# A tuned two-layer GELU block: early loads in order of need on one queue, remainder rows used last, first tiles copied ahead

**Chip, cores, metric.** One core of one Trainium2 chip. The time is the device time of one execution in microseconds (us); the profile's span is about 1.3 us shorter. Medians and ranges are of several executions. Times inside a profile are us from the start of its span.

## The reference

```python
B, S, D, F = 1, 2048, 448, 1792          # all bf16
def reference(x, w1, b1, w2, b2):
    h = jnp.einsum("bsd,df->bsf", x, w1) + b1
    h = gelu_tanh(h)
    return jnp.einsum("bsf,fd->bsd", h, w2) + b2
```

D = 448 is three tiles of 128 rows and a remainder of 64; F is 14 tiles ("F-tiles"). The remainder rows of w1 ("w1r") are a load of their own.

## The kernel before

The sequence is cut into four blocks of 512 rows. For the first block x is loaded as it is (two loads, `x(0)` and `x(2)`, of two tiles each) and turned by TensorE; the other blocks come through transposing loads. Layer 1 of the first block runs in two halves of 256 columns, each in seven steps of two F-tiles. A step has two parts, which use the two 64-row halves of the array crosswise; TensorE runs them in the order 0a, 1a, 0b, (b1 and tiles 2, 3 turned), 2a, 1b, 3a, 2b and so on. In the code, names such as `("w1r", 1)` are events that a load raises and a matmul waits for.

```python
W1CUTS = (0, 2, 6, 14)                       # w1 in chunks of 2, 4 and 8 F-tiles
load_x(0); load_w1(0); load_x(2); load_w1(1); load_w1(2)     # all issued on SyncE
load_w2(0, 7); load_w2(7, 14)
# ... b2, and 12 transposing loads for blocks 1 to 3, also on SyncE
load_w1r(0, 1, ("w1r", 0))                   # on ScalarE: for F-tiles 0, 1
load_w1r(1, NPAIR, ("w1r", 1))               # on ScalarE: the rest
# ... ScalarE's table load; GpSimd makes the identity and loads b1

def turn(t, engines):
    # VectorE: xr[t] = remainder columns of x, twice side by side   (after x)
    # TensorE: four transposes into PSUM, the fourth from xr[t]
    # VectorE: evacuation of the four into xT
    ...
# layer 1, one step (cut)
def part_a():
    for k in range(KT + 1):                  # k == KT is w1r: 8 matmuls
        for lo in (0, 1):
            after = need if k == 0 else []
            after = after + [("w1", w1_of(2 * j + lo)) if k < KT else ("w1r", min(j, 1))]
            mm(lo, lo, k, k == 0, False, after, turned if k == KT and lo else None)
def part_b():
    for k in range(KT):                      # 6 matmuls
        ...
# start
warm(7); turn(0, "vector"); turn(1, "vector"); warm(1)      # warm: matmuls on ones, for the clock
```

## Time and profile before

| | kernel before |
|---|---|
| time, first three executions | 102.14 us (102.1 to 102.41) |
| span of the profiled execution | 100.8 us |
| step 0 of layer 1 starts | 5.77 |
| second w1 chunk used first | 8.07 |
| w1r of the later steps used first | 9.90 |
| step 2 starts | 12.56 |
| layer 2 of the first block starts | 24.15 |
| half clock, as recorded | 10.03 to 16.86 |

How to read it: from 24.15 on TensorE runs without a gap, so a change at the start is worth exactly what it moves this point. The lines are in the prediction.

### The profile page before, as it was taken

Reading aid. Unit: us, or ns where it says so; the run is one execution under the profiler, and the core shown is the slowest. Engines: PE = TensorE matmul, PEld = TensorE weight load, DVE = VectorE, ACT = ScalarE, POOL = GpSimd, SP = SyncE. Lnnn points to the kernel's source line nnn. Section 1 sums busy time; section 2 is a strip of 40 time slices with the busy share of each in tenths; the row PEclk is TensorE's granted clock in tenths of the full one; section 3 lists DMA queues with packets and bytes.
Section 4 is the critical chain, followed back from the end, with each engine's and each line's share of the span. In section 5 each row is a group of like instructions: output and inputs, shape, how many; then the busy total and the mean of one; then the engine's idle time right before and its main releaser. Section 6 shows DMA issues by size and latency. Waiting matters only on the chain.

```text
span 100.8 us, 2247 instructions
## 1 busy us (share of the span) xinstructions
PE 94.4 (94%) x1020; PEld 51.3 (51%) x1020; DVE 12.4 (12%) x29; ACT 39.1 (39%) x73; POOL 2.4 (2%) x9
## 2 busy tenths in 40 slices
PE   6862899999999999999999999999999999999991
PEld 2411477887455444445455444445454444457790
DVE  0210310100001440000004500000034100000421
ACT  0500335999100018887000068891000388850001
POOL 6300000000000000000000000000000000000000
PEclk9999556999999999999999999999999999999999
DMA  2899999555520330000001210000002200000032
GB/s 60 216 291 361 380 287 160 66 106 102 65 48 0 95 94 0 0 3 0 7 0 46 90 47 0 7 0 0 7 0 91 91 0 7 0 0 0 0 98 91
DMA packets 13321, 7.34 MB, mean 73 GB/s; under 512 B 7936, under 2 KB 12928, under 8 KB 13312
## 3 DMA queue, kind: packets, MB, share of 16 engines
q1 hardware_dynamic: 12288, 6.97, 26.5%
q10 hardware_dynamic: 960, 0.23, 1.0%
q8 instruction: 8, 0.13, 0.6%
q0 software_dynamic: 64, 0.00, 0.0%
q14 instruction: 1, 0.01, 0.0%
HBM read 3.79 MB, written 1.84 MB: 56 GB/s over the span
## 4 chain that ended last, share of the span: by engine, by line
PE 87%; DMA 7%; ACTq 2%; DVE 1%; issue 0%
PE u L228 44%; PE u L276 42%; DMA w1r<-in_w_dram 7%; ACTq L128 2%; PE u L180 1%; DVE xT L187 0%; DVE out_sb L315 0%; PE u L194 0%; DVE xr L174 0%; DVE b_f L196 0%; PE u L283 0%
## 5 line engine op out<-in xcount | busy, mean ns | idle before, releaser
L248 ACT ACTIVATE g<-u,b_f 128x512 bf16<-128x512 f32 (+1 forms) x70 | 37.2, 600 | 47.6 <-PE u L228 41.0
L228 PE MATMUL u<-xT,w_sb 64*128 64x512 bf16 (+1 forms) x420 | 45.0, 349 | 1.4 <-DMA w_sb<-in_w_dram 1.3
L276 PE MATMUL u<-w_sb,g 64*128 64x448 bf16 (+1 forms) x504 | 43.2, 328 | 0.0
L276 PEld LDWEIGHTS u<-w_sb,g 64*128 64x128 bf16 x504 | 24.2, 94 | 18.5
L228 PEld LDWEIGHTS u<-xT,w_sb 64*128 64x128 bf16 x420 | 21.0, 99 | 19.4 <-DMA w_sb<-in_w_dram 1.7
L300 DVE TENSOR_TENSOR out_sb<-u,b_bc 128x448 bf16<-128x448 f32 x14 | 8.1, 619 | 67.9 <-PE u L276 67.9
L228 PE MATMUL u<-xT,w1r 64*128 64x512 bf16 (+1 forms) x70 | 12.3, 350 | 1.3 <-DMA w1r<-in_w_dram 1.3
L228 PEld LDWEIGHTS u<-xT,w1r 64*128 64x128 bf16 x70 | 3.6, 100 | 4.5 <-DMA w1r<-in_w_dram 1.6
L166 PE MATMUL u<-const-bfloat16-1.0 128*128 128x512 bf16 x8 | 3.8, 625 | 0.8 <-PEq L384 0.8
L318 ACT CAST out_sb<-u 128x224 bf16<-128x224 f32 x1 | 0.3, 346 | 9.0 <-PE u L276 9.0
L150 ACT ACT_TABLE_LOAD x1 | 1.3, 1283 | 3.3 <-issue 3.3
L166 PEld LDWEIGHTS u<-const-bfloat16-1.0 128*128 128x128 bf16 x8 | 1.0, 132 | 2.1 <-issue 2.1
L180 PE MATMUL u<-ident,xn 128*128 128x128 bf16 x12 | 2.0, 312 | 0.0
L187 DVE COPY xT<-u 128x512 bf16<-128x512 bf16 x4 | 1.7, 425 | 2.0 <-PE u L180 2.0
L180 PE MATMUL u<-ident,xr 128*128 128x128 bf16 x4 | 1.2, 292 | 0.6 <-DVE xr L174 0.6
L180 PEld LDWEIGHTS u<-ident,xn 128*128 128x128 bf16 x12 | 1.4, 139 | 0.6 <-issue 0.6
L360 DVE COPY xT<-xT 64x512 bf16<-64x512 bf16 x3 | 0.9, 289 | 5.7 <-DMA xT<-in_x_dram 5.7
L180 PEld LDWEIGHTS u<-ident,xr 128*128 128x128 bf16 x4 | 0.5, 114 | 1.4 <-DVE xr L174 1.4
L174 DVE COPY xr<-xn 128x128 bf16<-128x128 bf16 x4 | 0.7, 187 | 2.4 <-DMA xn<-in_x_dram 2.4
L196 DVE CAST b_f<-u 128x14 f32<-128x14 bf16 x1 | 0.2, 173 | 5.4 <-PE u L194 5.4
L308 DVE TENSOR_TENSOR out_sb<-u,b_bc 128x448 bf16<-128x448 f32 x1 | 0.6, 625 | 1.7 <-PE u L276 1.7
L158 POOL DMA_DIRECT2D b1n<-in_b_dram x1 | 0.7, 652 | 0.2 <-issue 0.2
(15 smaller groups left out, 3.4 us busy)
## 6 DMA issues: line engine op xcount, KB each, us to landing
out_dram<-out_sb SPq DMA_DIRECT2D x16, 112.0 KB, 1.7
w_sb<-in_w_dram SPq DMA_DIRECT2D x2, 784.0 KB, 9.8
w_sb<-in_w_dram SPq DMA_DIRECT2D x1, 768.0 KB, 7.7
xn<-in_x_dram SPq DMA_DIRECT2D x2, 224.0 KB, 3.7
w_sb<-in_w_dram SPq DMA_DIRECT2D x1, 384.0 KB, 5.8
w_sb<-in_w_dram SPq DMA_DIRECT2D x1, 192.0 KB, 2.8
w1r<-in_w_dram ACTq DMA_DIRECT2D x2, 96.0 KB, 6.3
xT<-in_x_dram SPq DMA_TRANSPOSE x12, 4.1
```

The costliest lines, as they stand in the source:

```text
L128: pr.dma("scalar", lambda e, lo=lo: e.dma_start(w1r[lo * H:(lo + 1) * H, j0:j1, :], w1rv[:, j0:j1, lo, :]), event)
L150: pr.op("scalar", lambda e: e.activation(junk[:, :], one, ACT.Gelu_apprx_tanh))
L158: pr.dma("gpsimd", lambda e: e.dma_start(b1n[0:NFT, :], b1.rearrange("(c p) -> c p", p=P)), "b1n", after=["b1z"])
L166: pr.op("tensor", lambda e: e.matmul(unit[3][:, 1, 0:cols], lhsT=ones_w, rhs=ones_m[:, 0:cols], start=True, stop=True))
L174: pr.op("vector", lambda e: e.tensor_copy(xr[:, t, :].rearrange("p (two h) -> p two h", two=2), xn[:, t, D3:D].unsqueeze(1).broadcast_to([ ...
L180: pr.op("tensor", lambda e, k=k, src=src: e.transpose(stage(t)[:, k * P:(k + 1) * P], src, ident[:, :]), after=need, event=("xt", t) if k ...
L187: return e.copy(o, i) if engines == "scalar" else e.tensor_copy(o, i)
L228: pr.op("tensor", lambda e: e.matmul(unit[u][:, lo, 0:n], lhsT=lhsT, rhs=rhs, start=first, stop=fin), after=after, event=event)
L248: pr.op("scalar", lambda e, lo=lo, ft=ft: e.activation(g[:, ft, c0:c1], unit[u][:, lo, 0:n], ACT.Gelu_apprx_tanh, bias=b1_f[:, ft:ft + 1], ...
L276: pr.op("tensor", lambda e: e.matmul(unit[u][:, lo, 0:n], lhsT=g[rows, ft, j * P:(j + 1) * P], rhs=w2_sb[rows, ft, d0:d0 + n], start=first ...
L300: pr.op("vector", lambda e, lo=lo, j=j: e.tensor_tensor(out=out_sb[:, j, :], in0=unit[u][:, lo, 0:D], in1=b2_bc[:, :], op=ALU.add), after= ...
L360: pr.op("vector", lambda e, cs=cs: e.tensor_copy(xT[0:H, KT, cs], xT[H:P, KT, cs]), after=[("xT", c + 1)], event=("xTd", c + 1))
```

## The change

All early loads go on the SyncE queue in the order in which TensorE needs them. w1r is no longer split by step, only by array half (the halves change places), comes behind the first six F-tiles, and is used last in a step's second part. The last w1 load, of eight F-tiles, becomes two of four. Both xr copies are made before the first evacuation. The b1 load and the one-row b2 load go from GpSimd to ScalarE. Core of the diff (renamed lines, some removed lines and the moved b2 load are cut):

```diff
-        W1CUTS = (0, 2, 6, 14)
+        W1CUTS = (0, 2, 6, 10, 14)
...
-        def load_w1r(j0, j1, event):
+        def load_w1r():
             for lo in (0, 1):
-                pr.dma("scalar", lambda e, lo=lo: e.dma_start(
-                    w1r[lo * H:(lo + 1) * H, j0:j1, :], w1rv[:, j0:j1, lo, :]), event)
+                pr.dma("sync", lambda e, lo=lo: e.dma_start(
+                    w1r[(1 - lo) * H:(2 - lo) * H, :, :], w1rv[:, :, lo, :]), "w1r")
...
         load_x(0)
         load_w1(0)
+        load_w1(1)
+        load_w1r()
         load_x(2)
-        load_w1(1)
         load_w1(2)
+        load_w1(3)
         load_w2(0, 7)
         load_w2(7, 14)
...
-        load_w1r(0, 1, ("w1r", 0))
-        load_w1r(1, NPAIR, ("w1r", 1))
...
-        pr.dma("gpsimd", lambda e: e.dma_start(b1n[0:NFT, :], b1.rearrange("(c p) -> c p", p=P)), "b1n",
+        pr.dma("scalar", lambda e: e.dma_start(b1n[0:NFT, :], b1.rearrange("(c p) -> c p", p=P)), "b1n",
                after=["b1z"])
...
+        def turn(tiles, copier):
+            for t in tiles:
+                ...  xr copy of tile t
+            for t in tiles:
+                ...  four transposes of tile t, then its evacuation
...
             def part_a():
+                for k in range(KT):
+                    for lo in (0, 1):
+                        after = (need if k == 0 else []) + [("w1", w1_of(2 * j + lo))]
+                        mm(lo, lo, k, k == 0, False, after, turned if k == KT - 1 and lo else None)
+
+            def part_b():
                 for k in range(KT + 1):
                     for lo in (0, 1):
-                        after = need if k == 0 else []
-                        after = after + [("w1", w1_of(2 * j + lo)) if k < KT else ("w1r", min(j, 1))]
-                        mm(lo, lo, k, k == 0, False, after, turned if k == KT and lo else None)
+                        fin = k == KT
+                        mm(lo, 1 - lo, k, False, fin, [turned] if k == 0 else ["w1r"] if fin else [],
+                           ("h", c, 2 * j + lo, c0) if fin else None)
...
-        turn(0, "vector")
-        turn(1, "vector")
+        turn((0, 1), "vector")
```

More of the change, by code (lines that the diff above doesn't have):

```diff
@@ L146, in bass_standalone__dense_activation_gelu__prompt_kernel @@
                     xT[:, slot, c * SC:(c + 1) * SC], x2[c * SC:(c + 1) * SC, d0:d0 + P], transpose=True), ("xT", c))
-        load_w1r(0, 1, ("w1r", 0))
-        load_w1r(1, NPAIR, ("w1r", 1))
-        pr.op("scalar", lambda e: e.activation(junk[:, :], one, ACT.Gelu_apprx_tanh))
         pr.op("gpsimd", lambda e: e.memset(ident[:, :], 0.0), event="ident0")
@@ L157, in bass_standalone__dense_activation_gelu__prompt_kernel @@
         pr.op("vector", lambda e: e.memset(b1n[:, :], 0.0), event="b1z")
-        pr.dma("gpsimd", lambda e: e.dma_start(b1n[0:NFT, :], b1.rearrange("(c p) -> c p", p=P)), "b1n",
+        pr.dma("scalar", lambda e: e.dma_start(b1n[0:NFT, :], b1.rearrange("(c p) -> c p", p=P)), "b1n",
                after=["b1z"])
+        pr.op("scalar", lambda e: e.activation(junk[:, :], one, ACT.Gelu_apprx_tanh))
         busy = {}
@@ L170, in stage, with evac @@
             return unit[t // 2][:, t % 2, 0:2 * P].bitcast(BF16)
-        def turn(t, engines):
-            a = t - t % 2
-            pr.op("vector", lambda e: e.tensor_copy(
-                xr[:, t, :].rearrange("p (two h) -> p two h", two=2),
-                xn[:, t, D3:D].unsqueeze(1).broadcast_to([P, 2, H])), after=[("x", a)], event=("xr", t))
-            for k in range(KT + 1):
-                src = xn[:, t, k * P:(k + 1) * P] if k < KT else xr[:, t, :]
-                need = ["ident", ("x", a)] if k < KT else [("xr", t)]
-                pr.op("tensor", lambda e, k=k, src=src: e.transpose(
-                    stage(t)[:, k * P:(k + 1) * P], src, ident[:, :]),
-                    after=need, event=("xt", t) if k == KT else None)
-            def evac(e):
-                o = xT[:, :, t * P:(t + 1) * P]
-                i = stage(t).rearrange("p (k s) -> p k s", k=KT + 1)
-                return e.copy(o, i) if engines == "scalar" else e.tensor_copy(o, i)
-            pr.op(engines, evac, after=[("xt", t)], event=("xT0", t))
-            busy[(t // 2, t % 2)] = ("xT0", t)
+        def turn(tiles, copier):
+            for t in tiles:
+                pr.op("vector", lambda e, t=t: e.tensor_copy(
+                    xr[:, t, :].rearrange("p (two h) -> p two h", two=2),
+                    xn[:, t, D3:D].unsqueeze(1).broadcast_to([P, 2, H])), after=[("x", t - t % 2)], event=("xr", t))
+            for t in tiles:
+                for k in range(KT + 1):
+                    src = xn[:, t, k * P:(k + 1) * P] if k < KT else xr[:, t, :]
+                    need = ["ident", ("x", t - t % 2)] if k < KT else [("xr", t)]
+                    pr.op("tensor", lambda e, t=t, k=k, src=src: e.transpose(
+                        stage(t)[:, k * P:(k + 1) * P], src, ident[:, :]),
+                        after=need, event=("xt", t) if k == KT else None)
+                def evac(e, t=t):
+                    o = xT[:, :, t * P:(t + 1) * P]
+                    i = stage(t).rearrange("p (k s) -> p k s", k=KT + 1)
+                    return e.copy(o, i) if copier == "scalar" else e.tensor_copy(o, i)
+                pr.op(copier, evac, after=[("xt", t)], event=("xT0", t))
+                busy[(t // 2, t % 2)] = ("xT0", t)
         def turn_b1():
@@ L233, in part_a @@
                 need += [("xT0", t) for t in range(c0 // P, c1 // P)] if c == 0 else [("xT", c), ("xTd", c)]
+                for k in range(KT):
[3 more added lines that the diff above has]
+            def part_b():
                 for k in range(KT + 1):
                     for lo in (0, 1):
-                        after = need if k == 0 else []
-                        after = after + [("w1", w1_of(2 * j + lo)) if k < KT else ("w1r", min(j, 1))]
-                        mm(lo, lo, k, k == 0, False, after, turned if k == KT and lo else None)
-            def part_b():
-                for k in range(KT):
-                    for lo in (0, 1):
-                        fin = k == KT - 1
-                        mm(lo, 1 - lo, k, False, fin, [turned] if k == 0 else [],
+                        fin = k == KT
+                        mm(lo, 1 - lo, k, False, fin, [turned] if k == 0 else ["w1r"] if fin else [],
                            ("h", c, 2 * j + lo, c0) if fin else None)
@@ L338, in bass_standalone__dense_activation_gelu__prompt_kernel @@
         pr.op("gpsimd", lambda e: e.memset(b2_z[:, :], 0.0), event="b2z0")
-        pr.dma("gpsimd", lambda e: e.dma_start(b2_z[H:H + 1, :], b2.unsqueeze(0)), "b2z", after=["b2z0"])
+        pr.dma("scalar", lambda e: e.dma_start(b2_z[H:H + 1, :], b2.unsqueeze(0)), "b2z", after=["b2z0"])
         warm(NWARM)
-        turn(0, "vector")
-        turn(1, "vector")
+        turn((0, 1), "vector")
         warm(NFILL)
@@ L348, in bass_standalone__dense_activation_gelu__prompt_kernel @@
                 turn_b1()
-                turn(2, "vector")
-                turn(3, "vector")
+                turn((2, 3), "vector")
         for j in range(NPAIR):
```

## The prediction

> **What bounds the kernel now.** I read the chain of waits first, then the groups, then the first 26 us in order of time. The chain:
>
> ```profile
> PE 87%; DMA 7%; ACTq 2%; DVE 1%; issue 0%
> PE u L228 44%; PE u L276 42%; DMA w1r<-in_w_dram 7%; ACTq L128 2%; PE u L180 1%; DVE xT L187 0%; DVE out_sb L315 0%; PE u L194 0%; DVE xr L174 0%; DVE b_f L196 0%; PE u L283 0%
> ```
>
> TensorE sets the end, but the first tenth of the span is the load of the w1 remainder rows (issued on the ScalarE queue, L128), and the matmuls hang behind it. From 24.3 us on the chain alternates between pieces of 10.58 us (layer 1, 98 matmuls) and 10.59 us (layer 2, 112), without a gap; the change has nothing to win there. The start, from the timeline (start, length, engine):
>
> ```profile
> 5.05 0.63 PE L166 MATMUL u<-const-bfloat16-1.0 128*128 128x512 bf16 x1
> 5.77 0.82 PE L228 MATMUL u<-xT,w_sb 64*128 64x256 bf16 x6
> 8.07 0.50 PE L228 MATMUL u<-xT,w_sb 64*128 64x256 bf16 x6 [1.29 <-DMA w_sb<-in_w_dram]
> 9.90 0.31 PE L228 MATMUL u<-xT,w1r 64*128 64x256 bf16 x2 [1.33 <-DMA w1r<-in_w_dram]
> 12.56 0.82 PE L228 MATMUL u<-xT,w_sb 64*128 64x256 bf16 x6
> 14.88 1.49 PE L228 MATMUL u<-xT,w_sb 64*128 64x256 bf16 x12
> 17.38 0.82 PE L228 MATMUL u<-xT,w_sb 64*128 64x256 bf16 x12
> 24.15 2.05 PE L276 MATMUL u<-w_sb,g 64*128 64x448 bf16 x20
> ```
>
> Two DMA waits of 1.3 us stand in the first two steps. Less obvious: twelve matmuls take 1.49 us at 14.88 and 0.82 us at 17.38. That is the clock (columns: PE, weight loads, DVE, ACT and POOL busy, then PEclk, DMA share, GB/s):
>
> ```profile
> 7.50:10.00 2.50, 0.60 (x8) 0.32 (x10) 0.00 (x0) 0.00 (x0) 0.00 (x0) 1.00 1.06 361
> 10.00:12.50 2.50, 2.15 (x17) 1.08 (x15) 0.80 (x4) 0.84 (x2) 0.00 (x0) 0.51 1.09 380
> 12.50:15.00 2.50, 2.50 (x25) 1.78 (x26) 0.42 (x1) 0.73 (x2) 0.00 (x0) 0.50 1.30 291
> 15.00:17.50 2.50, 2.50 (x34) 1.88 (x32) 0.00 (x0) 1.31 (x4) 0.00 (x0) 0.63 0.86 168
> ```
>
> After the idle stretch the clock is halved, and "busy" hides it. The trace's clock records give the edges: full from 6.62, half from 10.03 to 16.86, full afterwards. Before 6.62 there is no record (the view shows 1.00), yet the 0.63 us filler and the six matmuls in 0.82 us at 5.77, against 0.50 us for six at 8.07, show half clock there too. So the waits cost twice: their own time, and 6.83 us of half clock after them.
>
> **What the Trainium skill says.** (1) "TensorE: Matmul & The Clock Gate", Part 1: the clock is half or full, judged over free-running windows of 3413 ns. The trace agrees: the edges lie 3.41 and 6.83 us apart. So the grid here is 3.20, 6.62, 10.03, 13.44, 16.86. (2) "DMA: Bandwidth & Descriptors", Queues, rings and completion order: each engine takes turns between queue rows, packet by packet. The trace agrees: from 5.0 to 6.5 us the packets of the second w1 chunk (1024 B, 46 ns each) alternate with w1r's (256 B, 18 ns) almost one for one. (3) The same page, Issuing engines are not separate DMA queues: a second issuer saves only issue time. So moving w1r to SyncE should lose no bandwidth and gives the order back.
>
> **The change, part by part.** Times are from the span's start.
>
> 1. Copying ahead. Now the second xr copy comes behind the first evacuation (4.72), TensorE waits for it 0.30 us, the second evacuation ends at 5.71 and step 0 starts at 5.77. With both xr copies first (two of 0.19 from 3.37) the eight transposes run through from 3.72 at the 0.105 us pitch seen there and end near 4.75; evacuations 4.38 to 4.80 and 4.82 to 5.24 (0.42 each). Step 0 starts at 5.30: 0.47 us earlier.
>
> 2. Order of loads. SyncE issues every 0.46 to 0.5 us, so the second w1 chunk (F-tiles 2 to 5, 384 KB) is its third issue, at 1.66 instead of 2.18. Its first packets now came at 4.37, behind x(2) and sharing with w1r, its last at 7.20, and TensorE got it at 8.06. In the new order it follows chunk 0, whose packets end at 3.5: 384 packets over 16 engines are 24 each, times 46 ns is 1.1 us, so data to 4.6; with the 0.45 to 0.8 us from last packet to landing that the present loads show, it lands at 5.1 to 5.4. Then w1r: 896 packets, 56 per engine, times 18 ns is 1.0 us, data to 5.7, landed by about 6.3 (now 9.85). Then x(2): 8 per engine times 74 ns is 0.6 us; but both x loads have slow first packets (up to 1.5 us in the second), so landed 6.9 to 8.0, say 7.4. The two 4-tile chunks behind take 1.1 us each and land near 8.5 and 9.6.
>
> 3. w1r last. A step's first part shrinks from 8 to 6 matmuls, its second grows from 6 to 8; the count stays 14. Step 1's first part no longer needs w1r. Only the last pair of step 0's second part does. Steps 0a and 1a (three pairs each at half clock, 0.213 a pair, from 256 columns) run 5.30 to 5.94 and 5.94 to 6.58; 0b (four pairs) 6.58 to 7.05, w1r being there already.
>
> 4. b1 transpose and tiles 2, 3. Today it is 1.78 us from the b1 transpose (10.78) to step 2 (12.56), of which the second xr copy behind an evacuation is 0.7. In the new order: b1 transpose 7.05, b1 copy to 7.5, two xr copies to 7.9, last transpose near 8.0. Step 2 starts at about 8.15 if x(2) is there by 7.4: 4.4 us earlier than now.
>
> 5. Clock. In the window 3.20 to 6.62 TensorE would stream 0.72 (warm-up) + 0.85 (transposes) + 0.43 (filler) + 1.28 (0a, 1a) = 3.28 of 3.41 us. The present kernel streams about 2.85 there and gets full clock at 6.62; in 10.03 to 13.44 it streams about 2.45 and does not. So the new one gets it at 6.62 as well. In the next window it would stream 0.43 + 0.5 + 1.9, about 2.8 us, against 0.5 now, so it should keep the clock. Then the 174 matmuls from step 2 to the end of the first layer 1 take 12.43 steps of 14, each 0.765 us (the spacing of the twelves after 17.38): 9.5 us instead of 11.6. That is another 2.1 us.
>
> Sum: layer 2 starts at 8.15 + 9.5 = 17.65 instead of 24.15, 6.5 us earlier. I take off 0.3 for a unit not yet freed (the evacuation of tile 3 ends at about 8.9, when step 3 wants its unit, and the gelus at 0.384 us each, two a step, are just 0.77 against TensorE's 0.765). Everything after is the same gap-free chain. 102.14 - 6.2 = 95.9; with the lean of the rivals below I say **96.1**.
>
> Beside the path: b1 and b2 loads move from GpSimd to ScalarE. b1n is issued near 1.0, lands near 4, needed at 7.05; the table load (1.28 us) ends near 3, long before the first gelu at 7.6. The w2 load now ends at 14.4 and has three us to spare. The transposing loads of the second x block, now done by 18.76, are needed at 17.65 + 10.6 = 28.2. Both stay hidden.
>
> **The rivals.** (a) The wait moves on: w1r's small packets or x(2)'s slow ones hold step 2 until 9 to 9.5. For it: x(2) took 2.5 us for 0.6 us of packets; against: part of that lay beside w1r's traffic. It costs 0.5 to 1.3 us: 96.5 to 97.3. (b) The clock isn't granted at 6.62, or is lost at 10.03, because the second w1 chunk is late or the transposes count for less than I think. Half clock to 10.03 adds about 1.1 us (97), to 13.44 about 2.8 (98.7), and losing it from 10.03 to 16.86 about 3.4 (99.3). For it: 72% of a window did not release the clock, 84% did, and I must read my 96% the same way. (c) The loads are bound by bytes and the order gains little: against it, the engines are only 0.6 to 0.8 busy from 3.5 to 5.0, and by 5.0 they had moved 685 KB, almost the 704 KB that the first three loads need. If it were so, step 2 would start near 10.5 and the result be 98 to 99. (d) All of it is hidden anyway: against it, the chain itself goes through these waits.
>
> **Range and chances.** The good case (95.6 to 96.2) gets about 0.55, (a) 0.2, (b) 0.17, (c) 0.06. Hence 95.2 to 98.6. Two per cent faster is 100.1; even losing the clock stays below that, so faster 0.95, within 2% 0.04, slower 0.01.
>
> **What would show it.** Right: the first layer 2 matmul near 17.7 to 18; step 0 at 5.3; no wait of TensorE for w1 over 0.3 us; w1r landed before 7; clock records with full from about 6.6 and no half stretch after; the 7% of w1r gone from the chain. Wrong: a wait for x(2) over 1 us at the second pair of tiles (then a); a half-clock stretch after 10 us (then b); w1 chunk 1 landing after 6.5 (then c). A stall in the later blocks, for w2 or the transposed x, would mean that I took a load as hidden that isn't.

## The result

| | before | changed |
|---|---|---|
| median of four executions, same rounds | 102.12 us (101.0 to 102.41) | 98.35 us (97.79 to 98.94) |
| span of the profiled execution | 100.8 | 96.5 |
| layer 2 of the first block starts | 24.15 | 19.80 |

The ratio is 0.9651 (95% interval 0.9558 to 0.9744). A ratio is always the mean time of one kernel's fast runs over that of the other's fast runs of the same rounds, so not quite the ratio of the medians. The kernel is 3.5% faster; 98.35 lies inside 95.2 to 98.6, but near its upper end: I had expected a gain of 6.0 us and 3.8 came. The profiled executions differ by 4.3 us, as the changed kernel's is the fastest of its four.

The chain of waits of the changed kernel, by share of the span:

```profile
PE 90%; DMA 5%; SPq 1%; DVE 0%; issue 0%
PE u L228 45%; PE u L275 44%; DMA w_sb<-in_w_dram 5%; PE u L180 1%; SPq L121 0%; SPq L114 0%; DVE out_sb L314 0%; PE u L194 0%; PE u L282 0%
```

w1r is gone from it as intended; in its place stands another load, of w1 itself. The same chain in order of time (start, length, what) says which one:

```profile
1.66 5.28 DMA w_sb<-in_w_dram
...
6.98 1.62 PE u L228 x14
8.60 0.22 PE u L194
8.82 1.08 PE u L180 x8
9.91 10.06 PE u L228 x176
19.97 10.59 PE u L275 x112
```

The load issued at 1.66 is the second w1 chunk (F-tiles 2 to 5). It landed at 6.94, not at 5.1 to 5.4. TensorE's timeline:

```profile
4.19 0.38 PE L165 MATMUL u<-const-bfloat16-1.0 128*128 128x512 bf16 x1
5.02 0.50 PE L228 MATMUL u<-xT,w_sb 64*128 64x256 bf16 x6 [0.46 <-DVE xT L187]
6.98 1.32 PE L228 MATMUL u<-xT,w_sb 64*128 64x256 bf16 x12 [1.46 <-DMA w_sb<-in_w_dram]
8.21 0.40 PE L228 MATMUL u<-xT,w1r 64*128 64x256 bf16 x2
9.84 1.17 PE L228 MATMUL u<-xT,w_sb 64*128 64x256 bf16 x12
10.96 0.82 PE L228 MATMUL u<-xT,w_sb 64*128 64x256 bf16 x12
19.80 0.54 PE L275 MATMUL u<-w_sb,g 64*128 64x448 bf16 x4
```

Step 0 starts at 5.02 and ends by 5.5; then 1.46 us of waiting; and twelve matmuls at 6.98 take 1.32 us where twelve at 10.96 take 0.82. The clock again (busy columns as in the prediction, then PEclk, DMA share, GB/s):

```profile
5.00:7.18 2.18, 0.70 (x10) 0.43 (x12) 0.00 (x0) 0.00 (x0) 0.00 (x0) 1.00 1.11 265
7.18:10.59 3.41, 3.41 (x31) 1.96 (x29) 1.22 (x5) 0.84 (x2) 0.00 (x0) 0.50 1.07 336
10.59:14.00 3.41, 3.41 (x66) 3.01 (x64) 0.00 (x0) 2.84 (x8) 0.00 (x0) 1.00 1.09 379
```

One window of half clock stands behind the wait, where the kernel before had two. All four executions of the changed kernel have a mean granted clock of 0.982 or 0.983 (one window: 3.41 x 0.5 / 96.5 = 0.018). Those of the kernel before that have a record read 0.966 (two windows), a few 0.95 (three; such runs took 102.17 to 103.0).

Where did chunk 1 lose its time? The trace has every packet of a DMA. Packets started in each quarter of a us, over all 16 DMA engines, in the changed kernel (1024 B packets at this time are chunk 1; it has 384):

```
from us          3.00 3.25 3.50 3.75 4.00 4.25 4.50 4.75 5.00 5.25 5.50 5.75 6.00
chunk 0 (512 B)   168  111   10    0    0    0    0    0    0    0    0    0    0
chunk 1 (1024 B)    0    4   18   17   28   35   41   49   57   75   42   14    4
w1r (256 B)         0    0    0    0    0    0   13    3   26   36  138  207  233
engines busy     1.15 0.86 0.46 0.59 0.71 0.86 1.04 0.96 1.02 1.11 1.15 1.15 1.18
```

Chunk 1's first packets come at 3.3, close behind chunk 0's as predicted, but only on some of the engines; the others join one after another until about 4.7. This is an estimate from the counts, since the trace doesn't name a packet's engine, but each load has sixteen landing records, as many as there are engines: chunk 0's lie between 3.68 and 4.00, chunk 1's between 4.87 and 6.94. An engine that joins at 4.7 still has its 24 packets of 46 ns (1.1 us) to do. And not every packet takes 46 ns: 27 of the 384, begun between 3.5 and 4.9, took 0.11 to 1.15 us, 11.9 us together, while none of chunk 0's was slow. So the data end at 6.2 and not at 4.6. Engines stand half idle from 3.5 to 4.25, so bytes are not the limit.

### The profile page after: what moved, and what is told of

Read it like the earlier page. It is cut to its first block, busy times and chain, and to the rows that moved or that the text cites. A ratio compares the mean times of both kernels' runs of the same rounds, so it can differ in the third digit from the quotient of the medians.

```text
span 96.5 us, 2246 instructions
## 1 busy us (share of the span) xinstructions
PE 91.5 (95%) x1020; PEld 50.6 (52%) x1020; DVE 12.4 (13%) x29; ACT 38.9 (40%) x73; POOL 1.1 (1%) x7
## 4 chain that ended last, share of the span: by engine, by line
PE 90%; DMA 5%; SPq 1%; DVE 0%; issue 0%
PE u L228 45%; PE u L275 44%; DMA w_sb<-in_w_dram 5%; PE u L180 1%; SPq L121 0%; SPq L114 0%; DVE out_sb L314 0%; PE u L194 0%; PE u L282 0%
## 5 line engine op out<-in xcount | busy, mean ns | idle before, releaser
L228 PE MATMUL u<-xT,w_sb 64*128 64x512 bf16 (+1 forms) x420 | 42.5, 339 | 1.9 <-DMA w_sb<-in_w_dram 1.5
L228 PEld LDWEIGHTS u<-xT,w_sb 64*128 64x128 bf16 x420 | 20.5, 96 | 18.8 <-DMA w_sb<-in_w_dram 1.7
L228 PE MATMUL u<-xT,w1r 64*128 64x512 bf16 (+1 forms) x70 | 11.9, 337 | 0.0
L337 POOL MEMSET b_z<- 128x448 bf16 x1 | 0.5, 471 | 0.0
```

What stands on the lines that cost most here:

```text
L228: pr.op("tensor", lambda e: e.matmul(unit[u][:, lo, 0:n], lhsT=lhsT, rhs=rhs, start=first, stop=fin), after=after, event=event)
L337: pr.op("gpsimd", lambda e: e.memset(b2_z[:, :], 0.0), event="b2z0")
```

## The experiments

My theory after the result: chunk 1 is late because a load that is third in the queue begins late on part of the engines, and the wait for it costs twice, by itself and by a window of half clock. Rivals: the bytes or a slow stretch of time are the bound; the clock plays no part. Each run is timed against the kernel before in the same rounds; where I set kernels of different calls side by side I use their ratios, and the changed kernel itself was timed in a call of its own. The first four shared a chip with seven runs of the kernel before (median 101.63), the next four likewise (101.85), the last two with eleven (101.35).

### e1_fill: TensorE kept busy in the wait

```diff
             roll(layer1(0, j, 0, HC))
+            if j == 0:
+                warm(6)
             if j == 1:
```

> The changed kernel with six more filler matmuls (512 columns) between step 0's first part and step 1's, where TensorE waits 1.46 us for the second w1 chunk. Theory (the late chunk costs twice, its wait and one window of 3.41 us at half clock after it): no half-clock window after 7 us, step 2 about 0.8 us and layer 2 about 1.5 us earlier than in the changed kernel, 96.6 to 97.3 us. Rival (only the wait itself matters): the waits end where they did, 98.2 to 98.6. Risk: in an execution that is still at half clock at 5.5 us the fillers take 2.6 us and push step 1 back by a us.

Measured: 97.16 us (97.06 to 97.45), ratio 0.9532. All four runs have mean clock 0.999 or 1.0.

```profile
5.62 1.48 PE L165 MATMUL u<-const-bfloat16-1.0 128*128 128x512 bf16 x6
7.04 0.83 PE L228 MATMUL u<-xT,w_sb 64*128 64x256 bf16 x12
9.24 0.83 PE L228 MATMUL u<-xT,w_sb 64*128 64x256 bf16 x12
19.04 7.16 PE L275 MATMUL u<-w_sb,g 64*128 64x448 bf16 x74
```

Step 1 begins no earlier than before (7.04), but runs at full clock: twelve matmuls in 0.83 us. Work without use took 1.2% off the time (0.9651 to 0.9532; the intervals, 0.9558 to 0.9744 and 0.9464 to 0.9599, just overlap), and 97.16 lies in the theory's range. So the clock part of the theory holds; the rival that only the wait counts falls. In the profiles the gain is smaller than I had said: step 2 is 0.60 us earlier (9.24 instead of 9.84) and layer 2 0.76, not 0.8 and 1.5. The loads further back in the same queue took over: step 1's end waited for w1r (a line of the timeline), and then tiles 2, 3 could not be turned before x(2) had landed at 8.51 (two lines of the chain).

```profile
8.04 0.28 PE L228 MATMUL u<-xT,w1r 64*128 64x256 bf16 x2 [0.18 <-DMA w1r<-in_w_dram]
```

```profile
3.54 4.97 DMA xn<-in_x_dram
8.55 0.75 PE u L180 x8
```

### e2_merge: the first two w1 loads as one

```diff
-        W1CUTS = (0, 2, 6, 10, 14)
+        W1CUTS = (0, 6, 10, 14)
 ...
         load_x(0)
         load_w1(0)
-        load_w1(1)
         load_w1r()
         load_x(2)
-        load_w1(2)
-        load_w1(3)
+        load_w1(1)
+        load_w1(2)
```

> The changed kernel with the first two w1 chunks loaded as one (six F-tiles, 576 KB, rows of 1536 B), second in the queue. In the changed kernel the third load of the queue trickled from 3.5 to 4.8 us. Theory A (a load that comes third starts late on some of the DMA engines): the merged load starts near 2.6, lands at 4.8 to 5.4, step 0 starts at 5.3 and runs into step 1 without a wait; 96.0 to 96.8 us. Rival B (there is a slow stretch at 3.5 to 4.8 whatever is loaded, or bytes are the bound): it lands at 6.3 to 7, step 0 waits for it, and the time is 98 to 99.

Measured: 95.51 us (95.44 to 95.55), ratio 0.9364: the lowest ratio here (its interval, 0.93 to 0.9429, overlaps those of e3 and e9), and the steadiest times. The chain and TensorE's timeline:

```profile
1.19 4.17 DMA w_sb<-in_w_dram
```

```profile
5.50 1.39 PE L227 MATMUL u<-xT,w_sb 64*128 64x256 bf16 x18 [0.30 <-DMA w_sb<-in_w_dram]
6.71 0.28 PE L227 MATMUL u<-xT,w1r 64*128 64x256 bf16 x2
7.91 0.83 PE L227 MATMUL u<-xT,w_sb 64*128 64x256 bf16 x12
17.53 8.68 PE L274 MATMUL u<-w_sb,g 64*128 64x448 bf16 x90
```

Six F-tiles (576 KB) land at 5.36, earlier than the last four of them did as a load of their own (6.94). From 3.5 to 4.5 the DMA engines, half idle in the changed kernel, are full (62 to 65 packets of 1536 B per quarter us, share 1.02 to 1.06), so there is no slow stretch of time, and the bytes are the same: both forms of the rival fall. Step 2 starts at 7.91 and layer 2 at 17.53; the prediction had 8.15 and 17.65.

### e3_act: the second chunk on the ScalarE queue

```diff
-        load_w1(1)
+        load_w1(1, "scalar")          # issued before b1, at 0.75 us
```

> The changed kernel with the second w1 chunk issued on the ScalarE queue at about 0.75 us, beside x(0) and the first chunk on SyncE. Theory A (its late start is the wait in one queue's descriptor stream): its packets start before 3 us, it lands at 5 to 5.7, step 0 starts within 0.3 us of 5.0 to 5.3; 96.3 to 97.2 us. Rival B (the two queues get in each other's way as in the kernel before): lands at 6.5 or later and the first loads later too, 98 to 99.

Measured: 95.88 us (95.56 to 97.3, five runs), ratio 0.9397. In the profiled execution, which is a slow one (97.3), chunk 1 ran first, its packets from 2.5 to 4.2, and chunk 0, issued on SyncE, only after it, from 3.75 to 4.9:

```profile
6.00 2.10 PE L228 MATMUL u<-xT,w_sb 64*128 64x256 bf16 x18 [0.75 <-DMA w_sb<-in_w_dram]
```

So step 0 waits 0.75 us, step 1 not at all. My expectation of a start within 0.3 us of 5.0 to 5.3 missed; the gain came, and was larger than expected (96.3 to 97.2). This execution stayed at half clock until about 9.6 (eighteen matmuls in 2.10 us against 1.39 in the merged kernel). Its trace has no clock record at all and the mean clock reads 1.0, so this figure can't be trusted for time that no record covers.

### e4_turn: only the copies ahead

The kernel before with the new `turn` alone.

> The kernel before with only the new order of the copies (both xr copies ahead, for tiles 0, 1 and 2, 3). Theory: step 0 starts 0.45 us earlier but waits for the second w1 chunk and w1r as before (step 1 at 8.1, w1r at 9.9), so only the second pair's 0.5 to 0.7 us remains: 101.4 to 101.8 us. Rival (the copies are a good part of the gain of 3.8): below 101.

Measured: 100.4 us (99.51 to 101.67), ratio 0.9816 (0.9723 to 0.9909), unclear at 2%. Step 0 gained as expected, but the loads came differently in this execution: the second w1 chunk at 9.06, not 8.1, and w1r before it:

```profile
5.34 0.50 PE L229 MATMUL u<-xT,w_sb 64*128 64x256 bf16 x6
9.06 0.82 PE L229 MATMUL u<-xT,w_sb 64*128 64x256 bf16 x6 [2.71 <-DMA w_sb<-in_w_dram]
```

Step 0 starts 0.43 us earlier and TensorE waits longer. The time is lower than I expected, and by the number that I had set (below 101) the rival came. The profiled execution (99.51) has one half-clock window instead of two; the other three have two (0.966). So part of the gap to my expectation is the clock in one of the runs; that the other two fast runs (100.31 and 100.5) lie below my range as well stays unexplained. The interval reaches 0.9909; I don't read 1.8% as the worth of the copies. e10 measures it in the changed kernel.

### e5_split: the second chunk in two loads with short rows

```diff
-        W1CUTS = (0, 2, 6, 10, 14)
+        W1CUTS = (0, 2, 4, 6, 10, 14)
         load_w1(0)
         load_w1(1)
+        load_w1(2)
         load_w1r()
         load_x(2)
-        load_w1(2)
         load_w1(3)
+        load_w1(4)
```

> The changed kernel with the second w1 chunk (F-tiles 2 to 5, rows of 1024 B) loaded as two chunks with rows of 512 B, third and fourth in the queue. So far loads with rows of 1024 B and more ramped up slowly (x, chunk 1, the merged chunk), while chunk 0 and w1r, with 512 B and 256 B, did not. Theory R (the slow start goes with the long rows): F-tiles 2, 3 stream at once after chunk 0, data to about 4.2 us, landed by 4.9; step 1 starts with no wait over 0.3 us; 96.2 to 97.3 us. Theory P (the slow start goes with the third place in the queue): tiles 2, 3 trickle from 3.5 to 4.7 us, step 1 waits until about 5.8 to 6.3; 97 to 98.3 us.

Measured: 98.5 us (97.46 to 98.94), ratio 0.966, as the changed kernel, and 0.2 us above P's range. The third load, now of 512 B rows, trickles all the same: 44, 43 and 46 packets in the three quarters from 3.5, with the engines 0.34 to 0.44 busy, where chunk 0 had 168 in one. Theory R, long rows, falls; P stands. All this, and the lines below, is from the profiled execution, a slow one:

```profile
5.87 0.83 PE L229 MATMUL u<-xT,w_sb 64*128 64x256 bf16 x12 [0.47 <-DMA w_sb<-in_w_dram]
8.48 0.28 PE L229 MATMUL u<-xT,w1r 64*128 64x256 bf16 x2 [1.78 <-DMA w1r<-in_w_dram]
```

Step 1 starts 1.1 us earlier, at 5.87, as P said, but w1r has become the wait, 1.78 us: one more load ahead of it in the queue. Three of the four runs have lost a window of clock (0.982 or 0.983), the fastest (97.46) has not.

### e6_four: four F-tiles first, then w1r

```diff
-        W1CUTS = (0, 2, 6, 10, 14)
+        W1CUTS = (0, 4, 8, 14)
         load_w1(0)
-        load_w1(1)
         load_w1r()
         load_x(2)
+        load_w1(1)
         load_w1(2)
-        load_w1(3)
```

> An attempt to beat both: first w1 load of four F-tiles (384 KB), then w1r, x(2), four and six F-tiles. Step 0 then doesn't wait for w1 (landing 4.6 to 5.0, the copies end near 5.0 to 5.3), step 1 needs nothing more, and w1r is third. Theory: step 0 at 5.0 to 5.3, half clock nowhere after 7 us, layer 2 at 17.2 to 17.6; 94.9 to 95.5 us, at or below the merged kernel's 95.5. Rival (w1r or x(2) becomes the wait): 95.5 to 96.5.

Measured: 96.58 us (96.13 to 98.86), ratio 0.949. My range, 94.9 to 95.5, missed. Steps 0 and 1 wait for no load, but the chunks behind are late:

```profile
5.24 1.16 PE L227 MATMUL u<-xT,w_sb 64*128 64x256 bf16 x18 [0.45 <-DVE xT L186]
8.03 0.83 PE L227 MATMUL u<-xT,w_sb 64*128 64x256 bf16 x12 [0.33 <-DMA w_sb<-in_w_dram]
10.21 0.50 PE L227 MATMUL u<-xT,w_sb 64*128 64x256 bf16 x6 [0.49 <-DMA w_sb<-in_w_dram]
```

The wait moved, though to w1 itself and not to w1r or x(2) as the rival had it. Here w1r is third behind a second load that keeps the engines busy until about 4.1, and it starts at full rate (224 packets in the quarter from 4.0). A dip comes later instead: from 4.75 to 5.25 the engines are 0.78 to 0.80 busy.

### e7_w1rfirst: w1r in the first part again

The changed kernel with `part_a` and `part_b` as before (8 and 6 matmuls) and w1r stored to suit.

> The changed kernel with one part undone: w1r is used in the first part of each step again (8 and 6 matmuls), with the new loads. Theory (the late use of w1r hides its landing behind steps 0 and 1): step 0's last pair waits for w1r until about 8.2 us, steps 1 and 0b follow; layer 2 0.4 to 1.0 us later than in the changed kernel, 98.8 to 99.5 us. Rival (the place of w1r doesn't matter, as chunk 1 comes just before it): 98.0 to 98.6.

Measured: 99.65 us (98.35 to 100.02), ratio 0.9764.

```profile
5.33 0.82 PE L228 MATMUL u<-xT,w_sb 64*128 64x256 bf16 x6
8.05 0.40 PE L228 MATMUL u<-xT,w1r 64*128 64x256 bf16 x2 [1.89 <-DMA w1r<-in_w_dram]
```

As the theory said: chunk 1's matmuls queue behind the wait for w1r, so using w1r last is worth 1.1% here (0.9764 against 0.9651, with intervals that overlap, 0.9663 to 0.9866 and 0.9558 to 0.9744). The time is 0.15 us above my range. The profiled execution got full clock only at 13.58, so the 1.1% is not free of the clock.

### e8_swap: the first two w1 loads in the other order

```diff
-        load_w1(0)
         load_w1(1)
+        load_w1(0)
         load_w1r()
```

> The changed kernel with the first two w1 loads in the other order (F-tiles 2 to 5 second in the queue, tiles 0, 1 third): a look at the packets. Theory R (slow start with long rows): the chunk with 1024 B rows, now second, ramps up over half a us or more from about 2.5, and the 512 B rows, now third, stream at once behind it. Theory P (slow start in third place): the 1024 B rows stream at once, and the 512 B rows trickle until about 4.7.

Measured in one look: 96.05 us, 2.3 below the changed kernel's median, state unknown, as it is a single run. Packets per quarter us:

```
from us          2.50 2.75 3.00 3.25 3.50 3.75 4.00 4.25 4.50 4.75
chunk 1 (1024 B)   12   31   77   91   94   67   12    0    0    0
chunk 0 (512 B)     0    0    0    0    0   38  122  142   67   15
w1r (256 B)         0    0    0    0    0    0    0   15  149  210
```

```profile
5.68 1.21 PE L228 MATMUL u<-xT,w_sb 64*128 64x256 bf16 x18 [0.48 <-DMA w_sb<-in_w_dram]
```

Neither theory was quite right. The long rows, second, take from 2.5 to 3.25 to reach full rate, as R had it, but the engines are 1.03 to 1.06 busy meanwhile, with the end of x(0) until 3.0, and the chunk's slowest packet took 0.31 us, not 1.15. The third load doesn't trickle either, against P as I had put it. What fits the runs of the new order: the third load is slow to start on part of the engines if the second is so short that they run dry (at 3.4: the changed kernel, e1, e5, e7, e10), and is not if the second keeps them busy until about 4 (e2, e6, e8). Here too a dip comes later: the engines are 0.42 busy from 5.25 to 5.5. Whether the descriptors come late or an emptied engine restarts late isn't told apart by these runs.

### e9_b1early: the merged kernel with b1 turned ahead

```diff
         turn((0, 1), "vector")
         warm(NFILL)
+        turn_b1()
 ...
             if j == 1:
-                turn_b1()
                 turn((2, 3), "vector")
```

> The merged kernel (first w1 load of six F-tiles) with the b1 transpose moved ahead of step 0, where TensorE waits for w1 anyway. In the merged kernel the b1 copy stands on VectorE ahead of the xr copies of tiles 2, 3, and TensorE waits 0.3 us for them at 7.2 to 7.5. Theory: b1 leaves that chain, step 2 starts at 7.5 to 7.7 instead of 7.91, 95.1 to 95.3 us, ratio to the kernel before about 0.933. Rival (x(2) lands just then and the wait is its own): no change, 95.4 to 95.6.

Measured: 95.46 us (95.4 to 97.94), ratio 0.9427 (0.938 to 0.9473); its only slow run is 97.94. No change against the merged kernel's 95.51. The rival is right:

```profile
7.53 0.34 PE L179 MATMUL u<-ident,xn 128*128 128x128 bf16 x3 [0.22 <-DMA xn<-in_x_dram]
8.15 0.83 PE L227 MATMUL u<-xT,w_sb 64*128 64x256 bf16 x12
```

b1 has left the chain, and x(2) is now what TensorE waits for at that place. The two kernels' ratios differ more than their times because the kernel before happened to be faster in these rounds (101.35 against 101.63); the intervals overlap.

### e10_oldturn: the changed kernel with the old order of copies

> The changed kernel with the old order of the copies (each tile copied behind the evacuation of the one before), all else as changed. Theory (the copies ahead pay only where no load is waited for): step 0 starts 0.45 us later, hidden by the wait for the second w1 chunk, and the second pair of tiles takes 0.5 to 0.7 us longer: 98.6 to 99.2 us, ratio about 0.971. Rival (0.45 and 0.6 both count): 99.3 or more.

Measured: 98.96 us (97.74 to 101.0), ratio 0.9735.

```profile
5.77 0.50 PE L227 MATMUL u<-xT,w_sb 64*128 64x256 bf16 x6
7.28 0.83 PE L227 MATMUL u<-xT,w_sb 64*128 64x256 bf16 x12 [1.00 <-DMA w_sb<-in_w_dram]
10.56 0.82 PE L227 MATMUL u<-xT,w_sb 64*128 64x256 bf16 x6
```

Step 0 starts 0.75 us later than in the changed kernel's profile (0.45 against kernels at half clock there) and the wait behind it is shorter by 0.46. The copies ahead are worth 0.8% by the ratios (0.9735 against 0.9651), as expected, though the intervals overlap (0.9661 to 0.9808 and 0.9558 to 0.9744).

## Why the prediction was right in kind and too high in size

1. **Copying ahead**: right. Step 0 at 5.34 (e4) and 5.33 (e7) in executions at half clock until then, 5.30 predicted; 5.02 in the changed kernel's profile, which had full clock already.
2. **Order of loads**: the step that failed. It said that chunk 1's data would run "to 4.6" and land "at 5.1 to 5.4". It landed at 6.94. I took 24 packets of 46 ns behind chunk 0's end for all engines alike. Most packets have that length, but the engines began at different times between 3.3 and about 4.7, and 27 packets took up to 1.15 us. The loads behind it in the queue were late with it: x(2) landed at 8.69, not 7.4. The sign was in the profile before: the third load there, x(2), trickles over the same stretch with the engines 0.6 to 0.8 busy. I put that down to slow first packets of x and to w1r's traffic. e5 shows it with short rows of w1, and with no other queue that matters. One sum is wrong besides: the first three loads are 224 + 192 + 384 = 800 KB, not 704, so 685 KB by 5.0 was a weaker argument against (c) than it looked.
3. **w1r last**: right. w1r cost TensorE no idle time; only a weight load waited 0.4 us for it. It landed at 8.16, not 6.3, as it stood behind chunk 1; with steps 0 and 1 at full clock that is a small wait (0.18 us in e1). e7 shows that with the old use this would have been a wait of 1.89 us.
4. **b1 and tiles 2, 3**: 1.30 us from the b1 transpose (8.54) to step 2 (9.84), at half clock; 1.10 predicted.
5. **Clock**: failed with step 2. It said that the clock should be kept in the next window. It would have been, by e2. With the wait of 1.46 us TensorE was busy 0.70 of 2.18 us from 5.0 and lost the clock for a window; e1 gives it back with fillers, and with it 0.76 us in the profiles and 1.2% by the ratios. Two more errors did no harm. The streaming sums count the warm-up to the end of its last matmul (0.72 us), though the first transpose starts at 3.72 already; with 0.52 instead, 2.85 is 2.65 (78% of the window, not 84%) and 3.28 is 3.08. And I took the windows' grid from the profile before (3.20, 6.62, 10.03) as if it were tied to the start of the kernel. Full clock came at 3.76 in the changed kernel's profile, 4.10 in e1's, 6.01 in e2's and 13.58 in e7's. Much of the spread between executions of these kernels goes with how many windows fell to half.

The sum failed by the same term: step 2 at 9.84 instead of 8.15 (1.69 us), and layer 2 at 19.80 instead of 17.65 (2.15 us). Of the rivals, (b) came with its reason: a window lost because chunk 1 was late. (a) stood just behind it: with the clock kept (e1), w1r and x(2) are the next waits, and step 2 starts at 9.24. The sign named for (c), chunk 1 after 6.5, came without (c)'s reason: e2 and e8 load the same bytes, and TensorE waits 0.30 and 0.48 us for w1 instead of 1.46. The main sum (95.9) missed by 2.4 us; 98.35 lies in the range only because the rivals had widened it. With chunk 1 in time (e2) layer 2 starts at 17.53 and the time is 95.51, which the good case of the prediction put at 95.6 to 96.2. That is the strongest support for the rest of the sum.

**Left open**: why the third load begins late on part of the engines when the second is short, and how much of its delay is the slow packets. e8 is a single run. The move of w1r to SyncE, the new split of w1 and w1r, and the move of the b1 and b2 loads have no run of their own.

## What to carry to other kernels

As far as this shows: for the first loads of a kernel, put the big one where it can start while an earlier one still keeps the DMA engines busy, and don't cut off a small piece "for an early start" unless TensorE would really start earlier: here it was ready at 5.0 to 5.3 and six tiles in one load landed at 5.36. Count a wait at the start of a kernel with the clock it costs afterwards, and check with fillers how much that is. The mean granted clock doesn't show half clock ahead of the first record; matmul times do.

## What the Trainium skill lacked or had wrong

- "Perfetto Trace Analysis", DMA Optimizations, says that splitting DMAs may let the whole finish sooner where DMA engines are generally idle. It lacks the reverse case: here the engines were 0.46 to 0.86 busy from 3.5 to 4.5, so not idle in general, and one load instead of two (192 and 384 KB) landed at 5.36 instead of 6.94.
- "DMA: Bandwidth & Descriptors": I found in it no word on how a load's start spreads over the 16 engines. Here the third load of a queue, issued at 1.66, had landing records from 4.87 to 6.94 and 27 packets of 0.11 to 1.15 us when the second was 192 KB; behind a second load of 384 KB the third ran at full rate from about 4.0 (e6, e8).
- The same page, Issuing engines are not separate DMA queues, has a second issuer save only issue time. Putting one load on ScalarE (e3) gave 0.9397 against 0.9651, and its profile shows another load running second; order alone gave about the same (e8, a single run, 96.05 against 101.85: 0.943), so the sentence isn't contradicted, but it is easily read as "makes no difference".
- "TensorE: Matmul & The Clock Gate", Part 1, gives the window (3413 ns; the trace agrees) and says that it runs freely, which these runs agree with (first full clock at 3.76 to 13.58). It doesn't say how much work within a window keeps the clock. Estimated from streaming times here (at full clock 0.06 us a transpose, 0.22 a filler, 0.107 a pair of matmuls): about a third of a window lost it (changed kernel, 3.76 to 7.18: transposes, filler, step 0 and the start of step 1, 1.2 us), about half kept it (e5, 3.49 to 6.91: the same and all of step 1's first twelve, 1.8 us), and so did three quarters (e1, 4.10 to 7.51, with six fillers).
- The same section warns that clock records can be unreliable, but not that they may begin late: mean clock 1.0 in e7's profile, which was at half clock until 13.58, and in e3's, which has no record.
